# Attention steps laid between triples of matrix products, with order edges, and an add moved to the vector engine

## Chip, cores and metric

The kernel runs on one core of one Trainium2 chip. The metric is the device time of one execution in microseconds (us). Three runs of the kernel before took 760.43, 761.77 and 764.90 us, median 761.77 us.

## What is computed

The kernel chains three blocks on 1152 tokens (2 sequences of 576) of width 512.

1. Causal attention, 8 heads of width 64, with a bias from a running sum of `max(s, 0)`:
   `scores = q·kᵀ/8 + min(-(cum_i - cum_j), 0)`, masked above the diagonal; `attn = exp(scores - max) / (sum + 1e-9)`; `attn·v`.
2. A mixture of 4 experts: `out += p[:, e] * (relu(x @ w1[e]) @ w2[e])`, with w1 512x1024 and w2 1024x512.
3. A gated block: `((x @ w_a) * (x @ w_b)) @ w_out`, inner width 1536.

All in 32-bit floats. The kernel splits each operand of a product into a high and a low part and sums three products on TensorE (high·high, high·low, low·high). Such a group of three is a *triple*.

## The kernel before

**Stages.** The attention's rows fall into four groups (`GROUPS`, line 37): rows 0 to 255 of the first sequence, the rest of the first, the first 320 rows of the second, the rest of the second. The experts' tokens fall into turns (`TURNS`, line 41): 0 to 255, 256 to 511, 512 to 767, 768 to 1151. Three things are emitted in this order: the attention of group 0 with the first four steps of group 1 (line 1035); then `run(beside, True)` (line 1106), four expert stages (experts 0 and 1 on turn 0, expert 1 on turns 1 and 2) with the attention of groups 1 to 3 between them; then, with the attention closed, `run(after, False)`, which does all the rest: the last turn of expert 1 (products named `psq`), the other experts and the gated block.

**Experts' units.** A stage has 8 first-layer units (`l1_unit`, line 280: 4 triples of 256 columns into one PSUM bank, then ReLU and the two parts) and 2 second-layer units (`l2_unit`, line 292: 8 triples of 512 columns into one bank, then `add_share`). A triple is issued by `mm3` (line 255). The units are laid so that the first unit of the next stage comes ahead of the second layer of the stage before (`pipelined`, line 872).

**Attention steps.** `seq` (line 785) lists 80 pairs of head and row tile: steps 0 to 15 are group 0, 16 to 39 group 1, 40 to 63 group 2, 64 to 79 group 3. `attn_step` (line 792) number n is software-pipelined: it issues on TensorE the transposes of tile n-3 (L644), the scores of tile n (L596, L597), and, where a head ends, the product with v of the head that ended at n-4 (L680); beside it the softmax of tile n-1 (L606 on VectorE, L621 on ScalarE), the norm of tile n-2 (1e-9 added at L631 on ScalarE, or L629 on VectorE in group 0; reciprocal L632 on VectorE; multiplication L633 on GpSimd) and the copies of the transposed tile n-3 (L659 on ScalarE, L661 on VectorE). At a head's first step it also prepares the next head (L557 to L565) and issues the loads of the one after (L547 to L549) and of v (L571) on SyncE's queue, on which the weights' loads (L149) stand too.

**Pace.** `run` keeps a clock of the experts' products: a triple of n columns costs 3(n/2400 + 0.013) us, so a first-layer unit 1.44, a second-layer unit 5.43, a stage 22.35 and all four 89.4 us. After each unit it advances the clock, lays weight loads and splits (`weight_step`, one per 4 us of that clock), and then lays as many attention steps as `lead` (line 1077) asks for: steps 20 to 43 evenly by their column count over clock 0 to 29.7, steps 44 to 67 over 29.7 to 52.1, steps 68 to 83 over 52.1 to 74.4.

**Order in the queues.** The order laid in the program is a rank, not the queue's order. At compile time a scheduler with a timing model of its own fills each engine's queue: of the instructions that this model takes to be ready it takes the one laid first. So an attention instruction whose inputs are not ready in the model is passed by products laid behind it, as far as buffers reach (three PSUM banks for the experts' products). On the chip each queue then runs in the order that was written.

Of the kernel before, what the change touches and what calls it, by code (L numbers as in the profile page):

```python
# [11 lines left out]
AF = mybir.ActivationFunctionType  # L12
ALU = mybir.AluOpType
# [6 lines left out]
P = 128  # L20
# [26 lines left out]
NT0 = 256  # L47

NFIRST = 4


@with_exitstack
def fused_kernel(ctx, tc, qT, kT, v, s, dp, w1, w2, wa, wb, wo, out):
    nc = tc.nc
# [13 lines left out]
    ident = const.tile([P, P], F32, name="ident")  # L68
# [123 lines left out]
    def split_piece(r, key, form, wide, src, j):  # L192
# [16 lines left out]
        else:  # L209
            nsplit[0] += 1  # L210
            lo_eng = nc.gpsimd if nsplit[0] % 2 or nsplit[0] <= NFIRST else nc.vector
            two = slice(2 * j, 2 * j + 2)
# [39 lines left out]
    hts = {}  # L252
    begun = set()

    def mm3(ps, w, x, first, last, more=False):

        (lh, ll), (rh, rl) = w, x
        for k, (l, r) in enumerate(((lh, rh), (lh, rl), (ll, rh))):
            nc.tensor.matmul(  # L259
                ps, lhsT=l, rhs=r, start=first and k == 0, stop=last and k == 2, skip_group_check=more  # L260
            )

    def cols(pair, *at):
        return tuple(t[(slice(None), *at)] for t in pair)
# [320 lines left out]
    def st_scores(j, i):  # L585
        t = j.t[i]
        q0 = j.tiles[i][0] - j.q0
        cuts = [0, t.n] if t.n <= 512 else [0, 320, t.n]
        t.ps = []
        for c0, c1 in zip(cuts, cuts[1:]):  # L590
            ps = ps_s.tile([P, c1 - c0], F32, tag="sc", name=f"sc{j.nm}_{i}")
            t.ps.append((ps, c0, c1))
            if j.gi == 0:
                nc.tensor.matmul(ps, lhsT=j.qh[:, q0 : q0 + P], rhs=j.kr[:, c0:c1], start=True, stop=True)
                continue
            nc.tensor.matmul(ps, lhsT=j.qh[:, q0 : q0 + P], rhs=j.ks[:, c0:c1], start=True, stop=False)  # L596
            nc.tensor.matmul(ps, lhsT=j.qb[:, q0 : q0 + P], rhs=j.kb[:, c0:c1], start=False, stop=True)  # L597

    def st_softmax(j, i):
        t = j.t[i]  # L600
# [24 lines left out]
    def st_norm(j, i):  # L625
        t = j.t[i]
        r = st_p.tile([P, 1], F32, tag="r", name="r")
        if j.gi == 0:
            nc.vector.tensor_scalar(out=t.l, in0=t.l, scalar1=1e-9, scalar2=None, op0=ALU.add)  # L629
        else:  # L630
            nc.scalar.activation(out=t.l, in_=t.l, func=AF.Copy, bias=1e-9)  # L631
        nc.vector.reciprocal(out=r, in_=t.l)  # L632
        (nc.gpsimd if j.gi else nc.vector).tensor_scalar(  # L633
            out=t.e, in0=t.e, scalar1=r, scalar2=1.0, op0=ALU.mult, op1=ALU.mult
        )

    def st_transpose(j, i):
        t = j.t[i]
        t.tp = []
        for c0, c1 in [(0, i + 1)] if i < 4 else [(0, 4), (4, 5)]:  # L640
            ps = ps_t.tile([P, c1 - c0, P], F32, tag="tr", name=f"tr{j.nm}_{i}")
            for c in range(c0, c1):
                k0 = j.tiles[c][0]
                nc.tensor.transpose(ps[:, c - c0, :], t.e[:, k0 : k0 + P], ident)  # L644
            t.tp.append((ps, c0, c1))

    def st_evac(j, i):
        t = j.t[i]
# [19 lines left out]
    def st_av(j):  # L668
        a = (j.h % 2) * D
        if j.gi == 0 and j.h % 2:  # L670
            ps = xpair[j.gi]
        else:
            ps = ps_a.tile([P, j.nr], F32, tag="av", name=f"av{j.nm}")
        mms = []
        for c in range(j.i1):
            o = max(0, j.tiles[c][1] - j.r0)
            for e in (j.eh, j.el) if j.gi else (j.eh,):
                mms.append((c, o, e))
        for m, (c, o, e) in enumerate(mms):
            nc.tensor.matmul(  # L680
                ps[:, o:] if j.gi else ps[a : a + D, o:],
                lhsT=j.vs[:, c, :],
                rhs=e[:, c, o:],
                start=(m == 0),
                stop=(m == len(mms) - 1),
            )
        c = D - a
        t0 = j.b * S + j.r0
        x = slice(t0, t0 + j.nr)
        if j.gi == 0:  # L690
            xpair[j.gi] = ps
            if j.h % 2:
                split(xh[j.h // 2][:, x], xl[j.h // 2][:, x], ps, nc.vector)
            return
        if j.h % 2 == 0:
            xpair[j.gi] = (
                x_p.tile([P, j.nr], F32, tag="xs", name="xs"),
                x_p.tile([P, j.nr], F32, tag="xt", name="xt"),
            )
        xs, xt = xpair[j.gi]  # L700
        nc.scalar.activation(out=xt[a : a + D, :], in_=ps[c : c + D, :], func=AF.Copy)
        nc.vector.tensor_tensor(  # L702
            out=xs[a : a + D, :], in0=ps[a : a + D, :], in1=xt[a : a + D, :], op=ALU.add
        )
        if j.h % 2 == 1:
            split(xh[j.h // 2][:, x], xl[j.h // 2][:, x], xs, nc.gpsimd)
# [8 lines left out]
    c0 = st_p.tile([NR, 1], F32, tag="c0", name="c0")  # L715
# [15 lines left out]
        out=cum[:, :NT0], data0=ones[:NR, :NT0], data1=sc[:, :NT0], initial=0.0,  # L731
        op0=ALU.mult, op1=ALU.add,
# [5 lines left out]
        out=causal[:, S - P :], in_=causal[:, S - P :], pattern=[[-1, P]], compare_op=ALU.is_ge, fill=MASKED,  # L738
# [6 lines left out]
    for base, cm in ((0, 1), (H - 1, -1)):  # L745
        nc.gpsimd.affine_select(
            out=pick, in_=pick, pattern=[[-cm * H, len(GROUPS)]], compare_op=ALU.is_ge, fill=0.0,
# [4 lines left out]
        out=cum[:, NT0:], data0=ones[:NR, NT0:], data1=sc[:, NT0:], initial=cum[:, NT0 - 1 : NT0],  # L752
        op0=ALU.mult, op1=ALU.add,
    )
    nc.vector.tensor_tensor_reduce(
        out=pick, in0=cum[:, D : D + 4 * P].rearrange("p (g c) -> p g c", c=P)[:, :, D],
# [8 lines left out]
    for j_ in range(3):  # L765
        in_order(nc.sync.dma_start(
            out=ckD[j_].rearrange("g h c -> (g h) c"), in_=ck3[j_].bitcast(F32)
# [18 lines left out]
    state = {"n": 0}  # L786
# [5 lines left out]
    def attn_step():  # L792
        n = state["n"]
        state["n"] += 1

        if x := at(n):
            j, i = x
            if i == j.i0:
                k = jobs.index(j)
                if k + 1 < len(jobs):  # L800
                    prep_job(jobs[k + 1])
                if k + 2 < len(jobs):
                    load_job(jobs[k + 2])
            st_enter(j, i)
        if x := at(n - 3):
            st_transpose(*x)
        if x := at(n):
            st_scores(*x)
        if x := at(n - 2):
            st_norm(*x)  # L810
        if x := at(n - 1):
            st_softmax(*x)
        if x := at(n - 4):
            j, i = x
            if i == j.i1 - 1:
                st_av(j)
        if x := at(n - 3):
            st_evac(*x)
        if x := at(n):
            j, i = x  # L820
            if i == j.i0:
                prep_v(j)
                k = jobs.index(j)
                if k + 1 < len(jobs):
                    load_v(jobs[k + 1])
# [6 lines left out]
    def close_attention():  # L832
        actx.close()
        open_pools(ctx, [("h2", 2), ("raw", 3), ("q", 2), ("cv", 1)])
        pools["late"] = True
        late_ps.append(ctx.enter_context(tc.tile_pool(name="ps_m2", bufs=5, space=PSUM)))
        for part_ in ("h", "l"):
            tq[part_] = ctx.enter_context(tc.tile_pool(name="tq" + part_, bufs=1)).tile(
                [P, 3, 2, SL], F32R, name="tq" + part_
            )  # L840
# [211 lines left out]
    n = [k for k, u in enumerate(after) if u[0] == ("w1", halves[1][1])][-1]  # L1052
# [11 lines left out]
    area = [0]  # L1064
# [5 lines left out]
    for n in (2, 3, 4):  # L1070
        us = sum(c for st in stages[:n] for part in expert_stage(*st) for _, c, _ in part)
        turn_t.append(us)
    SLACK = 15.0
    lead = []
    for g in range(3):
        u0 = lead[-1][1] if lead else 0.0
# [2 lines left out]
    PACE, LATE_PACE = 4.0, 3.0  # L1079
    clock = {"t": 0.0, "w": 0.0}  # L1080

    def run(units, attention):
        for k, cost, u in units:
            for key in keys_of(k):
                weights_to(key)
            u()
            for key in keys_of(k):
                used(key)
            if hold[0]:
                continue  # L1090
            clock["t"] += cost
            while clock["w"] < clock["t"]:
                clock["w"] += PACE if attention else LATE_PACE
                weight_step()
            if not attention:
                continue
            goal = state["n"]
            for u0, u1, s0, s1 in lead:
                if u0 < clock["t"]:
                    c = area[s0] + (area[s1] - area[s0]) * min(1.0, (clock["t"] - u0) / (u1 - u0))  # L1100
                    while goal < s1 and area[goal + 1] <= c + 1e-6:
                        goal += 1
            while state["n"] < goal:
                attn_step()

    run(beside, True)
    close_attention()
    run(after, False)


# [48 lines left out]
```

## Time and profile before

| | |
|---|---|
| median of three runs | 761.77 us |
| the profiled execution | 760.76 us |
| its span, first to last instruction | 759.0 us |
| TensorE (PE) busy | 719.9 us, 95% |
| VectorE (DVE) busy | 533.0 us, 70% |
| ScalarE (ACT) busy | 334.8 us, 44% |
| GpSimd (POOL) busy | 416.2 us, 55% |
| mean granted TensorE clock | 0.987 of full speed |

The profile is of one execution; 1.8 us lie outside its span. PE is TensorE's matmuls, PEld its weight loads, which overlap them. PEclk is the clock that TensorE was granted, 1.00 being 2.4 GHz and 0.50 being 1.2 GHz; a value between is a mean over a stretch that has both. In a row of the timeline or of a group, `ps<-wh,hh` names the tile written and the tiles read; `sc` is the scores, `tr` the transposes, `av` the product with v, `ps` the experts' products up to the end of the attention.

### The profile page before, as it was taken

Reading aid. Unit: us, or ns where it says so; the run is one execution under the profiler, and the core shown is the slowest. Engines: PE = TensorE matmul, PEld = TensorE weight load, DVE = VectorE, ACT = ScalarE, POOL = GpSimd, SP = SyncE. Lnnn points to the kernel's source line nnn. Section 1 sums busy time; section 2 is a strip of 40 time slices with the busy share of each in tenths; the row PEclk is TensorE's granted clock in tenths of the full one; section 3 lists DMA queues with packets and bytes.
Section 4 is the critical chain, followed back from the end, with each engine's and each line's share of the span. In section 5 each row is a group of like instructions: output and inputs, shape, how many; then the busy total and the mean of one; then the engine's idle time right before and its main releaser. Section 6 shows DMA issues by size and latency. Waiting matters only on the chain.

```text
span 759.0 us, 11106 instructions
## 1 busy us (share of the span) xinstructions
PE 719.9 (95%) x3868; PEld 630.9 (83%) x3868; DVE 533.0 (70%) x1119; ACT 334.8 (44%) x756; POOL 416.2 (55%) x330
## 2 busy tenths in 40 slices
PE   5979897997998999999999999999899999999997
PEld 3678886886978888888888888888788888898896
DVE  7656857757759777776556657679874788887764
ACT  4667748868864432223312323243645324242410
POOL 1777735647634754333313344598466878788600
PEclk9999998999998999999999999999999999999999
DMA  6457323324402131211001112122102132213003
GB/s 192 136 184 228 91 68 90 100 74 127 120 18 84 55 100 41 81 57 57 31 25 56 56 57 74 65 84 87 53 29 86 62 103 68 95 63 104 5 1 125
DMA packets 35095, 61.34 MB, mean 81 GB/s; under 512 B 3472, under 2 KB 19376, under 8 KB 35040
## 3 DMA queue, kind: packets, MB, share of 16 engines
q1 hardware_dynamic: 34864, 60.50, 24.8%
q8 instruction: 31, 0.51, 0.3%
q14 instruction: 24, 0.20, 0.1%
q10 hardware_dynamic: 176, 0.14, 0.1%
HBM read 55.02 MB, written 2.58 MB: 76 GB/s over the span
## 4 chain that ended last, share of the span: by engine, by line
PE 55%; DVE 12%; POOL 8%; issue 4%; ACT 2%; DMA 1%; POOLq 0%; ACTq 0%; DVEq 0%; SPq 0%
PE ps L259 27%; PE psq L259 20%; PE pst L259 4%; POOL wl L74 3%; PE av L680 2%; POOL tp L155 1%; DVE tp L167 1%; PE tr L644 1%; DVE tp L163 1%; DVE h2l L74 1%; DVE acc L1027 1%; DVE tp L159 1%; POOL t L155 1%; DVE t L167 1%; DVE psq L405 1%
## 5 line engine op out<-in xcount | busy, mean ns | idle before, releaser
L259 PE MATMUL ps<-wh,h2h 128*128 128x512 f32 x332 | 130.6, 393 | 0.0
L259 PE MATMUL ps<-wl,h2h 128*128 128x512 f32 x332 | 129.6, 390 | 0.0
L74 POOL TENSOR_TENSOR wl<-raw,wh 128x1024 fp32r<-128x1024 f32 x24 | 58.5, 2448 | 125.5 <-ACT wh L73 95.4
L259 PE MATMUL ps<-wh,h2l 128*128 128x512 f32 x332 | 125.7, 392 | 0.8 <-DVE h2l L74 0.8
L307 DVE SCALAR_TENSOR_TENSOR acc<-ps,pr,acc 128x512 f32<-128x512 f32 x111 | 82.1, 745 | 40.4 <-PE ps L259 39.7
L259 PE MATMUL psq<-xh,wh 128*128 128x448 f32 (+1 forms) x224 | 82.9, 372 | 1.7 <-DVE xs L702 1.7
L259 PE MATMUL psq<-xl,wh 128*128 128x448 f32 (+1 forms) x224 | 82.6, 369 | 0.0
L259 PE MATMUL psq<-xh,wl 128*128 128x448 f32 (+1 forms) x224 | 82.6, 370 | 0.0
L259 PEld LDWEIGHTS ps<-wh,h2l 128*128 128x128 f32 x332 | 62.2, 188 | 14.7 <-DVE h2l L74 1.6
L259 PEld LDWEIGHTS ps<-wh,h2h 128*128 128x128 f32 x332 | 62.4, 188 | 11.8 <-ACT h2h L73 0.3
L259 PEld LDWEIGHTS ps<-wl,h2h 128*128 128x128 f32 x332 | 62.4, 188 | 11.1
L318 ACT ACTIVATE h2h<-psq 128x448 fp32r<-128x448 f32 (+1 forms) x56 | 29.5, 532 | 93.6 <-PE psq L259 74.3
L74 POOL TENSOR_TENSOR wl<-sums,wh 128x1024 fp32r<-128x1024 f32 x24 | 58.6, 2441 | 5.2 <-ACT h2h L318 2.7
L73 ACT ACTIVATE wh<-raw 128x1024 fp32r<-128x1024 f32 x24 | 25.5, 1062 | 69.7 <-PE ps L259 52.9
L633 POOL TENSOR_SCALAR e<-e,r 128x448 f32<-128x448 f32 (+4 forms) x64 | 39.9, 630 | 28.9 <-DVE r L632 27.5
L259 PE MATMUL psq<-tqh,wh 128*128 128x448 f32 x144 | 52.9, 368 | 0.9 <-DVE h2l L74 0.5
L606 DVE CUSTOM_DVE_ANT_0 e<-sc,causal 128x128 f32<-128x128 f32 (+3 forms) x80 | 35.6, 450 | 24.2 <-PE tr L644 13.8
L259 PE MATMUL psq<-tql,wh 128*128 128x448 f32 x144 | 52.6, 365 | 0.0
L259 PE MATMUL psq<-tqh,wl 128*128 128x448 f32 x144 | 52.5, 364 | 0.0
L621 ACT ACTIVATE e<-e,mn 128x128 f32<-128x128 f32 (+4 forms) x80 | 45.9, 574 | 11.6 <-DVE mn L606 9.1
L644 PE MATMUL tr<-ident,e 128*128 128x128 f32 x240 | 45.2, 291 | 6.1 <-DVE el L661 4.1
L155 POOL TENSOR_SCALAR tp<-tp 128x512 f32<-128x512 f32 x24 | 47.4, 1995 | 5.9 <-ACT tp L154 5.9
(174 smaller groups left out, 1949.4 us busy)
## 6 DMA issues: line engine op xcount, KB each, us to landing
raw<-in_w SPq DMA_DIRECT2D x40, 512.0 KB
raw<-in_wa SPq DMA_DIRECT2D x12, 512.0 KB
raw<-in_wb SPq DMA_DIRECT2D x12, 512.0 KB
raw<-in_wo SPq DMA_DIRECT2D x12, 512.0 KB
kr<-in_kT SPq DMA_DIRECT2D x16, 288.0 KB
vr<-in_v SPq DMA_DIRECT2D x16, 160.0 KB
kb<-ks SPq DMA_DIRECT2D x16, 144.0 KB
out<-acc SPq DMA_DIRECT2D x9, 256.0 KB
```

The source lines that it names most:

```text
L73: nc.scalar.activation(out=hi, in_=src, func=AF.Copy)
L74: lo_eng.tensor_tensor(out=lo, in0=src, in1=hi.bitcast(F32), op=ALU.subtract)
L155: nc.gpsimd.tensor_scalar(out=t.bitcast(F32), in0=t.bitcast(F32), scalar1=2.0**-15, scalar2=GMAX, op0=ALU.max, op1=ALU.min,)
L167: nc.vector.scalar_tensor_tensor(out=t, in0=hi, scalar=-(1 << 30), in1=t, op0=ALU.bitwise_and, op1=ALU.bitwise_or,)
L259: nc.tensor.matmul(ps, lhsT=l, rhs=r, start=first and k == 0, stop=last and k == 2, skip_group_check=more)
L307: nc.vector.scalar_tensor_tensor(out=dst, in0=ps, scalar=share, in1=dst, op0=ALU.mult, op1=ALU.add)
L318: nc.scalar.activation(out=hh, in_=src, func=AF.Relu)
L606: nc.vector.tensor_tensor_reduce(out=t.e[:, c0:c1], in0=ps, in1=causal[:, m0 + c0 : m0 + c1], scale=-1.0, scalar=seed, op0=ALU.add, op1=AL ...
L621: nc.scalar.activation(out=t.e, in_=t.e, func=AF.Exp, bias=mn, scale=-1.0 if j.gi else -SCALE, accum_out=t.l)
L633: (nc.gpsimd if j.gi else nc.vector).tensor_scalar(out=t.e, in0=t.e, scalar1=r, scalar2=1.0, op0=ALU.mult, op1=ALU.mult)
L644: nc.tensor.transpose(ps[:, c - c0, :], t.e[:, k0 : k0 + P], ident)
L680: nc.tensor.matmul(ps[:, o:] if j.gi else ps[a : a + D, o:], lhsT=j.vs[:, c, :], rhs=e[:, c, o:], start=(m == 0), stop=(m == len(mms) - 1),)
```

## The change

- `run` no longer lays attention steps after a unit. Instead `mm3` itself advances the clock after each triple (`advance`) and lays the steps that are due there, in the middle of a unit. The cost of a triple and `lead` are as before.
- Each attention step records the names of its TensorE instructions: the second scores product, the last transpose, the last product with v. The first product of each later triple gets an order edge behind the instructions recorded by the third-last step laid (`LAG = 2`). The edge is on one engine and only fixes the order in its queue: no semaphore, no instruction.
- The recording and the edges end with `run(beside, True)`.
- In `st_norm` the 1e-9 is added on VectorE for all row tiles, not on ScalarE for groups 1 to 3.

```diff
+LAG = 2
...
+    passed, mixed = [], []
+    NOSYNC = mybir.DependencyInfo(mybir.DependencyClass.NoSync, mybir.DependencyReason.DATA)
+
     def mm3(ps, w, x, first, last, more=False):

         (lh, ll), (rh, rl) = w, x
         for k, (l, r) in enumerate(((lh, rh), (lh, rl), (ll, rh))):
-            nc.tensor.matmul(
+            ins = nc.tensor.matmul(
                 ps, lhsT=l, rhs=r, start=first and k == 0, stop=last and k == 2, skip_group_check=more
             )
+            if k == 0 and len(passed) > LAG:
+                for name in passed[-1 - LAG]:
+                    tc.add_manual_dep(ins.ins, name, NOSYNC, reason="the attention's pace")
+        if mixed:
+            mixed[0](3 * (rh.shape[-1] / 2400 + 0.013))
...
-            nc.tensor.matmul(ps, lhsT=j.qb[:, q0 : q0 + P], rhs=j.kb[:, c0:c1], start=False, stop=True)
+            ins = nc.tensor.matmul(ps, lhsT=j.qb[:, q0 : q0 + P], rhs=j.kb[:, c0:c1], start=False, stop=True)
+            passed[-1].append(ins.ins.name)
...
-        if j.gi == 0:
-            nc.vector.tensor_scalar(out=t.l, in0=t.l, scalar1=1e-9, scalar2=None, op0=ALU.add)
-        else:
-            nc.scalar.activation(out=t.l, in_=t.l, func=AF.Copy, bias=1e-9)
+        nc.vector.tensor_scalar(out=t.l, in0=t.l, scalar1=1e-9, scalar2=None, op0=ALU.add)
...
     def attn_step():
         n = state["n"]
         state["n"] += 1
+        passed.append([])
...
+    def advance(us):
+
+        clock["t"] += us
+        goal = state["n"]
+        for u0, u1, s0, s1 in lead:
+            if u0 < clock["t"]:
+                c = area[s0] + (area[s1] - area[s0]) * min(1.0, (clock["t"] - u0) / (u1 - u0))
+                while goal < s1 and area[goal + 1] <= c + 1e-6:
+                    goal += 1
+        while state["n"] < goal:
+            attn_step()
+
     def run(units, attention):
...
-            clock["t"] += cost
+            if not attention:
+                clock["t"] += cost
...
+    mixed.append(advance)
     run(beside, True)
+    mixed.clear()
+    passed.clear()
     close_attention()
```

## Rows read from the trace of the kernel before

**Rows 1.** The page: share of busy time, and the TensorE clock in 40 slices.
```profile
PE 719.9 (95%) x3868; PEld 630.9 (83%) x3868; DVE 533.0 (70%) x1119; ACT 334.8 (44%) x756; POOL 416.2 (55%) x330
...
PEclk9999998999998999999999999999999999999999
```

**Rows 2.** Stretches: length, busy PE, PEld, DVE, ACT, POOL, clock, DMA share.
```profile
20.00:62.40 42.40, 36.89 (x213) 30.31 (x212) 27.69 (x92) 27.18 (x74) 32.41 (x29) 0.96 0.54 173
62.40:113.70 51.30, 49.18 (x325) 44.89 (x324) 34.82 (x97) 34.07 (x93) 30.61 (x32) 1.00 0.36 111
113.70:140.60 26.90, 21.71 (x130) 18.77 (x128) 20.09 (x70) 22.78 (x80) 15.41 (x24) 0.87 0.31 89
140.60:169.80 29.20, 29.20 (x201) 26.75 (x200) 18.89 (x69) 20.26 (x77) 14.55 (x24) 1.00 0.30 87
169.80:197.90 28.10, 22.74 (x164) 20.09 (x164) 21.41 (x73) 25.09 (x79) 20.55 (x24) 1.00 0.46 131
197.90:231.50 33.60, 30.01 (x196) 26.30 (x195) 20.92 (x57) 20.16 (x54) 13.52 (x17) 0.99 0.16 43
```

**Rows 3.** The same view, two stretches that begin with the attention's last products.
```profile
220.00:240.00 20.00, 16.32 (x86) 14.79 (x85) 15.73 (x31) 8.20 (x21) 4.15 (x5) 0.83 0.27 87
...
233.00:500.00 267.00, 267.00 (x1314) 235.54 (x1314) 180.20 (x288) 84.51 (x126) 118.63 (x56) 0.99 0.18 60
```

**Rows 4.** TensorE's timeline at the attention's end: start, us, instruction, idle before it.
```profile
224.40 0.36 PE L680 MATMUL av<-eh,vs 128*128 128x256 f32 x1 [0.94 <-ACT eh L659]
...
231.59 0.69 PE L259 MATMUL psq<-xh,wh 128*128 128x384 f32 x1 [1.71 <-DVE xs L702]
232.08 0.52 PE L259 MATMUL psq<-xl,wh 128*128 128x384 f32 x1
...
239.15 0.34 PE L259 MATMUL psq<-xh,wh 128*128 128x384 f32 x1
```

**Rows 5.** TensorE's groups up to 62.4 us: experts' first products of triples, scores.
```profile
L259 PE MATMUL ps<-xh,wh 128*128 128x256 f32 x34 | 10.2, 342 | 3.2 <-DVE hl L287 3.2
...
L596 PE MATMUL sc<-ks,qh 128*128 128x320 f32 (+2 forms) x8 | 2.8, 352 | 0.0
...
L259 PE MATMUL ps<-wh,hh 128*128 128x512 f32 x6 | 2.3, 389 | 0.0
```

**Rows 6.** The same view from 62.4 to 113.7 us.
```profile
L259 PE MATMUL ps<-xh,wh 128*128 128x256 f32 x36 | 10.4, 292 | 0.8 <-DVE hl L287 0.8
L259 PE MATMUL ps<-wh,hh 128*128 128x512 f32 x26 | 10.3, 397 | 0.0
...
L596 PE MATMUL sc<-ks,qh 128*128 128x320 f32 (+2 forms) x20 | 7.2, 360 | 1.3 <-DVE mn L606 1.2
```

**Rows 7.** The same view from 140.6 to 169.8 us.
```profile
L259 PE MATMUL ps<-xh,wh 128*128 128x256 f32 x26 | 7.4, 285 | 0.0
...
L259 PE MATMUL ps<-wh,hh 128*128 128x512 f32 x16 | 6.3, 395 | 0.0
...
L597 PE MATMUL sc<-kb,qb 67*128 67x128 f32 (+2 forms) x12 | 3.4, 285 | 0.0
```

**Rows 8.** The same view from 169.8 to 197.9 us.
```profile
L596 PE MATMUL sc<-ks,qh 128*128 128x320 f32 (+2 forms) x16 | 5.6, 370 | 1.7 <-POOL ks L564 0.7 <-POOL vs L74 0.6 <-DVE mn L606 0.3
...
L259 PE MATMUL ps<-xh,wh 128*128 128x256 f32 x19 | 4.8, 287 | 0.0
```

**Rows 9.** The add by line: duration ns min/median/max; then VectorE's group of line 287.
```profile
L629 DVE TENSOR_SCALAR l<-l x16: 126/146/155, 11.9 to 34.3; 128x1 f32<-128x1 f32 x16
...
L631 ACT ACTIVATE l<-l x64: 184/197/232, 38.6 to 220.7; 128x1 f32<-128x1 f32 x64
...
L287 DVE SCALAR_TENSOR_TENSOR hl<-ps,hh 128x256 fp32r<-128x256 f32 x29 | 11.8, 417 | 1.6 <-ACT hh L286 1.0
```

**Rows 10.** Timelines of GpSimd and TensorE: one tile's norm, and its transposes.
```profile
90.76 0.64 POOL L633 TENSOR_SCALAR e<-e,r 128x448 f32<-128x448 f32 x1 [1.05 <-DVE r L632]
...
104.06 0.62 PE L644 MATMUL tr<-ident,e 128*128 128x128 f32 x4
```

**Rows 11.** SyncE's queue: weight loads ahead of a head's key load.
```profile
41.74 6.54 SPq L149 DMA_DIRECT2D raw<-in_w  x3
48.38 0.38 SPq L548 DMA_DIRECT2D kr<-in_kT  x1
```

**Rows 12.** TensorE's timeline in the first unit: products of one bank, out of program order.
```profile
25.84 0.70 PE L259 MATMUL ps<-xl,wh 128*128 128x256 f32 x3
...
29.24 0.71 PE L259 MATMUL ps<-xh,wh 128*128 128x256 f32 x3
```

More of the change, by code (lines that the diff above doesn't have):

```diff
@@ L643, in st_transpose @@
                 k0 = j.tiles[c][0]
-                nc.tensor.transpose(ps[:, c - c0, :], t.e[:, k0 : k0 + P], ident)
+                ins = nc.tensor.transpose(ps[:, c - c0, :], t.e[:, k0 : k0 + P], ident)
             t.tp.append((ps, c0, c1))
+        passed[-1].append(ins.ins.name)
     def st_evac(j, i):
@@ L679, in st_av @@
         for m, (c, o, e) in enumerate(mms):
-            nc.tensor.matmul(
+            ins = nc.tensor.matmul(
                 ps[:, o:] if j.gi else ps[a : a + D, o:],
@@ L686, in st_av @@
             )
+        passed[-1].append(ins.ins.name)
         c = D - a
@@ L1094, in run @@
                 weight_step()
[L1095 to L1104, printed above, removed]
+    mixed.append(advance)
     run(beside, True)
+    mixed.clear()
+    passed.clear()
     close_attention()
```

## The prediction, made before the change was run

> **What bounds the kernel now.** I read the page first, then TensorE's stretches, the groups of each stretch, and the timelines around the gaps. The page says TensorE is busy 95% of the span [rows 1], so what can be won is its idle time and its half-speed clock. From 233 to 500 us it is busy 267.00 of 267.00 us [rows 3]: whatever is gained before the attention's end reaches the end of the kernel in full. After that point the weights' chain follows TensorE's release of buffers, so I let it move along and cost nothing.
>
> The stretches [rows 2] are cut where the attention and the experts change roles. Up to 113.7 us the experts run ahead of the attention. By 62.4 us, when step 22 issues its scores, 34 triples of 256 columns and 6 of 512 are done [rows 5]; at the code's own price (0.120 and 0.226 us a product) that is 34x3x0.120 + 6x3x0.226 = 16.3 us of products, where the pace lays step 24 at 7.1 (column count 2368 of 9856, times 29.7 us). In the next stretch they do 36 and 26 more [rows 6], 13.0 + 17.6 = 30.6 us, beside 20 scores products, that is 15 steps. Then the experts have nothing left that does not need the attention's rows, and from 113.7 to 140.6 us the attention runs nearly alone: PE is busy 21.71 of 26.90 us at a mean clock of 0.87 [rows 2]. The same comes back from 169.8 to 197.9 us (22.74 of 28.10), and at the end the attention's tail stands alone, with 1.71 us of waiting for its last copy [rows 4]; the first products of the last turn then run at 1.2 GHz (one each 0.32 us, from 232.08 on; the row at 239.15 is at full speed), clock 0.83 over 220 to 240 us [rows 3, 4].
>
> The attention is late because of the order in TensorE's queue, and not because its data are late: a tile normed at 91.40 us is transposed at 104.06 [rows 10], with PE busy 49.18 of 51.30 us and no other engine above 68% [rows 2].
>
> **The change part by part.** All sums are against the profiled execution, 760.8 us, 1.0 below the median of 761.8.
>
> *The handovers go.* With the edges no triple may start before the third-last step's products have been issued, so the experts lead by two or three steps at most; by the pace 15 us of products (89.4 - 74.4) are left when the attention ends, which cover its tail. What can go at most: idle 5.2 + 5.4 + 3.6 us in the three handovers (length less PE busy [rows 2]), clock (1 - 0.87)x26.9 = 3.5 and (1 - 0.83)x20 = 3.4 us [rows 2, 3]. Sum 21.1 us. I take all of it, and charge what the pace costs separately. What is late next in each handover is the attention step itself.
>
> *The early hold.* At 62.4 us the experts may stand at 7.1 and not at 16.3 us, so up to 9.2 us of products are pushed out of a stretch in which step 22 comes no sooner: its head's key load stood on SyncE's queue behind three weight loads that took 6.54 us [rows 11], and POOL was busy 32.41 of 42.40 us [rows 2]. The edge binds only the first of a triple's three products. The others of an open bank may still pass, as the first unit shows, where three products of the second kind run ahead of three of the first [rows 12]; in a 512-column unit that is up to 16x0.226 = 3.6 us, in a 256-column one 1.0 us. Bounds 0 (the attention comes as much sooner as the experts are held) and 9.2; I take 7, the upper end less the mean of the two allowances (2.3).
>
> *The paced middle of group 1, steps 22 to 43.* TensorE's work per step: (49.18 - 30.6)/15 = 1.24 us for the attention [rows 2, 6] and 29.7/24 = 1.24 for the experts, 2.48 in all. VectorE's: 34.82/15 = 2.32, plus the add of 0.15 [rows 9], less 0.12 for the 0.8 us fewer products (half of them first-layer, one 0.417 us copy for each 1.44 us [rows 9]) = 2.35. No engine works without gaps where the attention sets the pace: the busiest one there, ACT, reached 22.78/26.90 = 0.85 and 25.09/28.10 = 0.89 [rows 2]. At 0.87 VectorE needs 2.70 us a step, so PE waits 0.22 a step, 22 steps: 4.8 us. Bounds: 0 (TensorE is the slower), and 20.7 (a step as slow as in the stretch now, 51.3/15 = 3.42). I take 4.8, because the transposes' wait for the queue [rows 10] is what goes away.
>
> *Group 2, steps 44 to 67.* TensorE: (29.20 - 26x3x0.120 - 16x3x0.226)/12 = 0.75 [rows 2, 7], plus 22.35/24 = 0.93: 1.68. VectorE: 18.89/12 = 1.57, plus 0.15, less 0.11: 1.61, at 0.87 1.85. 0.17x24 = 4.1 us; bounds 0 and, with the present 29.2/12 = 2.43 a step, 18.0.
>
> *Group 3, steps 68 to 83.* TensorE: (22.74 - 19x3x0.120)/10 = 1.59 (16 scores products are 10 to 11 steps [rows 8]), plus 22.35/16 = 1.40: 2.99. VectorE: 2.14 + 0.15 + 0.11 more for the products = 2.40, at 0.87 2.76. TensorE is the slower: 0. Bound above: at the share that VectorE itself reached there, 21.41/28.10 = 0.76, it needs 3.16, and 0.17x16 = 2.7 us.
>
> *The add.* It takes 64x0.197 = 12.6 us from ACT and gives VectorE 64x0.146 = 9.3 [rows 9]; its price is in the two terms above. Left on ACT, VectorE would need 2.53 and 1.68 us a step and ACT (34.07/15 - 0.11)/0.87 = 2.48 and (20.26/12 - 0.10)/0.87 = 1.83: waits of 1.1 and 3.6 us in place of 4.8 and 4.1. The Trainium skill (Perfetto Trace Analysis, Optimizing Scalar/DVE Operations) advises the opposite direction, from VectorE to ScalarE, where VectorE is saturated; by that rule this edit alone gives 4.2 us away. VectorE is at 68% in the stretch from 62.4 us and ACT at 66% [rows 2], so the trace of before does not say yet that VectorE is the saturated one.
>
> *At nothing:* the edges (no instruction), and the moved steps' DMAs: five per head on SyncE's queue, now half a unit sooner beside the weights' loads, with the DMA engines at 0.16 to 0.46 from 62.4 us on [rows 2]. They hide behind the head that is computed meanwhile; without that cover a held key load costs what the early hold shows. Weight steps stay at the ends of units.
>
> Sum: 21.1 - 7 - 4.8 - 4.1 = 5.2 us gained, 760.8 - 5.2 = 755.6, at the median 756.6.
>
> **Rivals.** (a) *TensorE starves behind the edges.* Its queue is in order, so a triple behind a late transpose waits with it, and with it all experts' work. If a step of group 1 stays at 3.42 us, that term is 20.7 and not 4.8, and the time is 756.6 + 15.9 = 772.5. It decides from 3.10 us a step on (0.40x22 = 8.9 us more, 765.5). For it: the queues of VectorE, ACT and POOL are ordered by a model that had the attention late; POOL at 76% and the held load early on [rows 2, 11]. Against: 12.7 us between norm and transpose [rows 10].
>
> (b) *Gain and price cancel.* The full 9.2 early, and engines at 0.83 in place of 0.87: 2.83 and 1.94 a step, 7.7 and 6.2 us. 21.1 - 9.2 - 7.7 - 6.2 = -2.0, about 763.8. The same comes out if the two unbound products of each triple let the experts pass as now; then 761.8.
>
> (c) *The pace costs nothing once group 1 is under way*, because the three engines do fill up: 21.1 - 7 = 14.1, 747.7. For it: DVE's share of 0.68 at present leaves room. Against: no stretch of the attention has any engine beside TensorE above 0.89.
>
> **How the numbers follow.** Chances: forecast 0.34, (a) 0.30, (b) 0.22, (c) 0.14. A measurement of this kernel tells about 0.5% (3.8 us) from no change. The forecast and (c) are faster: 0.48; (b) is the same: 0.22; (a) is slower: 0.30. The range runs from a little under (c)'s time to that of (a), 744 to 772; the likeliest case's own range is 750 to 760, its two wait terms halved or one of them doubled.
>
> **What would show it.** Right: by 62.4 us the experts have done some 8 us of products; between 113 and 200 us no stretch in which PE is below 85% busy; 12 to 15 us of `ps` products after the last `av`; no idle before the first `psq` and its clock at 1.00; gaps before `ps` of under 0.5 us each, spread over 60 to 160 us and released by VectorE or ACT. Wrong: a step of group 1 over 3.1 us with PE idle before transposes or scores (a); the experts again 10 us ahead at 113 us (b); clock rows at 0.5 inside the paced stretch, which would add 1.7 us for each 3.4 us.

## The result, and the profile after

The changed kernel takes 751.14 us (median of 4 runs, 749.86 to 753.25), the kernel before 761.1 in the same series: ratio 0.9875, 95% interval 0.9835 to 0.9915. Once more, beside other kernels: 0.9867 (0.9835 to 0.9899). The forecast of 756.6 us had the sign, the main mechanism (the handovers fill up) and half of the gain: 5.2 us forecast, 10.0 measured. The profiled execution took 749.86 us, 10.9 less than the one before; its span is 748.0 us.

The page first: shares of busy time, and the clock in 40 slices.

```profile
PE 714.3 (95%) x3868; PEld 628.3 (84%) x3868; DVE 538.7 (72%) x1183; ACT 329.6 (44%) x692; POOL 414.6 (55%) x330
...
PEclk9789999999999999999999999999999999999999
```

VectorE has 64 instructions more and ScalarE 64 fewer, which is the add [rows 1]. The slices with a clock under 0.9 have moved to the first 56 us. Then TensorE by the stretches of before, the last one cut where the attention's neighbours end (length; busy PE, PEld, DVE, ACT, POOL; clock; DMA share).

```profile
20.00:62.40 42.40, 36.36 (x204) 29.41 (x203) 34.55 (x116) 30.80 (x81) 36.86 (x32) 0.84 0.56 178
62.40:113.70 51.30, 44.35 (x278) 40.03 (x278) 38.73 (x121) 37.24 (x90) 35.44 (x37) 0.93 0.44 130
113.70:140.60 26.90, 26.90 (x197) 25.27 (x196) 23.18 (x103) 22.83 (x79) 17.89 (x30) 1.00 0.38 102
140.60:169.80 29.20, 27.96 (x211) 26.47 (x211) 22.68 (x87) 25.04 (x72) 20.00 (x26) 1.00 0.45 125
169.80:197.90 28.10, 28.10 (x189) 25.72 (x189) 20.12 (x70) 19.96 (x51) 15.96 (x20) 1.00 0.31 85
197.90:223.00 25.10, 23.78 (x153) 21.33 (x152) 18.78 (x40) 10.05 (x24) 4.84 (x6) 1.00 0.22 70
```

Against [rows 2] it reads like an exchange. The two handovers in the middle are gone: 26.90 of 26.90 us with 197 matmuls where 21.71 with 130 stood, and 28.10 of 28.10. In their place the stretch up to 62.4 us has a clock of 0.84 (0.96 before), and the stretch from 62.4 to 113.7 us has 6.95 us of idle TensorE where it had 2.12, and a clock of 0.93. The attention's end, TensorE's timeline (start, us, instruction):

```profile
221.76 0.39 PE L264 MATMUL ps<-wh,hl 128*128 128x512 f32 x1
221.99 0.34 PE L264 MATMUL psq<-xh,wh 128*128 128x384 f32 x1
222.17 0.34 PE L264 MATMUL psq<-xl,wh 128*128 128x384 f32 x1
```

The first product of the last turn starts at 221.99 us and not at 231.59, without a gap and at 2.4 GHz (0.18 us from start to start; before, 0.32 [rows 4]). The last product with v is at 211.9 us, so 10 us of products covered its copies. Up to there 9.6 us are gained and the half-speed start behind it is another 3.4. Of these 13.0 us the profiled execution gives 2.1 back in the rest of the kernel; 1.0 is a single longer wait (1.30 us before a `psq` product at 543.95, where it was 0.30), the remainder is spread and not explained.

Two groups say where the experts stand: first products of triples, and scores products, up to the scores of step 40 (109.5 us).

```profile
L264 PE MATMUL ps<-xh,wh 128*128 128x256 f32 x49 | 16.3, 332 | 0.0
L606 PE MATMUL sc<-ks,qh 128*128 128x320 f32 (+2 forms) x32 | 11.2, 358 | 2.7 <-POOL ks L574 2.7
L264 PE MATMUL ps<-wh,hh 128*128 128x512 f32 x16 | 6.7, 420 | 0.0
```

The same 32 scores products had 70 and 32 triples beside them in the kernel before, up to 121.6 us. At the code's price that is 28.5 us of products against 46.9: 18.4 us were kept for later.

What TensorE waits for now, from 20 to 223 us (line waited for: us in total, times, longest):

```profile
PE tr L652 <- DVE l L639: 4.0, 2, 2.9
PE sc L606 <- POOL ks L574: 2.7, 1, 2.7
PE sc L607 <- DMA kb<-ks: 2.4, 2, 2.1
PE tr L652 <- DVE el L670: 2.2, 6, 0.6
...
PE av L689 <- ACT eh L668: 1.6, 2, 1.2
```

The longest, 2.93 us, in the timelines of TensorE, VectorE and ScalarE:

```profile
97.68 0.52 PE L652 MATMUL tr<-ident,e 128*128 128x128 f32 x3 [2.93 <-DVE l L639]
...
93.84 2.44 DVE L222 TENSOR_TENSOR wl<-raw,wh 128x512 fp32r<-128x512 f32 x2 [2.44 <-ACT wh L220]
96.20 0.74 DVE L315 TENSOR_SCALAR acc<-ps,pr 128x512 f32<-128x512 f32 x1
96.86 0.68 DVE L670 TENSOR_TENSOR el<-tr,eh 128x512 fp32r<-128x512 f32 x1
97.46 0.14 DVE L639 TENSOR_SCALAR l<-l 128x1 f32<-128x1 f32 x1
...
97.78 0.28 DVE L640 RECIPROCAL r<-l 128x1 f32<-128x1 f32 x2
...
91.81 1.99 ACT L220 ACTIVATE wh<-raw 128x1024 fp32r<-128x1024 f32 x2
```

VectorE stood idle for 2.44 us until ScalarE had the high part of a weight, split the weight for 2.44 us, and only then came to an expert's sum and to the copy (L670) of the tile transposed before, which frees that tile's PSUM. The profile names the add of 1e-9 (L639) as what ended the wait. It runs at 97.46 us, right behind that copy, and the reciprocal that uses its result starts at 97.78, after the transposes have begun at 97.68. So it can't be their input, and I take the copy for what they waited for. This wait is weights' work lying in front of the attention's in a queue, not an engine that is full: VectorE is busy 38.73 of 51.30 us there, 0.755. The next two (2.7 us for a head's key on GpSimd, 2.1 for its DMA) are the preparation of a head.

### The profile page after: what moved, and what is told of

Its sections match the earlier page's. It is cut to its first block, busy times and chain, and to the rows that moved or that the text cites. A ratio compares the mean times of both kernels' runs of the same rounds, so it can differ in the third digit from the quotient of the medians.

```text
span 748.0 us, 11127 instructions
## 1 busy us (share of the span) xinstructions
PE 714.3 (95%) x3868; PEld 628.3 (84%) x3868; DVE 538.7 (72%) x1183; ACT 329.6 (44%) x692; POOL 414.6 (55%) x330
## 4 chain that ended last, share of the span: by engine, by line
PE 75%; DVE 11%; POOL 5%; DMA 4%; issue 3%; ACT 2%; SPq 0%; POOLq 0%; ACTq 0%; DVEq 0%
PE ps L264 35%; PE psq L264 24%; PE pst L264 6%; PE av L689 4%; PE tr L652 3%; POOL wl L76 2%; PE sc L604 1%; DMA raw<-in_w 1%; PE sc L607 1%; PE sc L606 1%; DMA kb<-ks 1%; POOL t L157 1%; POOL tp L157 1%; DVE t L169 1%; DMA kr<-in_kT 1%
## 5 line engine op out<-in xcount | busy, mean ns | idle before, releaser
L264 PEld LDWEIGHTS ps<-wh,h2h 128*128 128x128 f32 x332 | 62.4, 188 | 11.9 <-ACT h2h L75 0.4
L264 PEld LDWEIGHTS ps<-wl,h2h 128*128 128x128 f32 x332 | 62.4, 188 | 11.0
L264 PE MATMUL pst<-xh,wh 128*128 128x256 f32 x160 | 45.3, 283 | 2.7 <-DVE xl L76 2.7
```

The costliest lines, as they stand in the source:

```text
L264: ins = nc.tensor.matmul(ps, lhsT=l, rhs=r, start=first and k == 0, stop=last and k == 2, skip_group_check=more)
```

## The experiments

Each is measured against the kernel before, run beside it. For "lead" I counted the experts' products queued ahead of a step's scores, at the code's price, less the clock at which the pace lays that step; the kernel before has 12 us at step 22, 19 at step 40, 23 at step 64. "Reaches the last turn" is the start of the first `psq`.

**The add alone.**

```diff
-        if j.gi == 0:
-            nc.vector.tensor_scalar(out=t.l, in0=t.l, scalar1=1e-9, scalar2=None, op0=ALU.add)
-        else:
-            nc.scalar.activation(out=t.l, in_=t.l, func=AF.Copy, bias=1e-9)
+        nc.vector.tensor_scalar(out=t.l, in0=t.l, scalar1=1e-9, scalar2=None, op0=ALU.add)
```

> The kernel before with the 1e-9 added on VectorE for all row tiles; nothing else changed. My theory (the order of TensorE's queue carries the gain; the attention waits for that queue and not for VectorE or ScalarE) expects no change that can be measured: 757 to 765 us, with the experts still about 10 us of products ahead at step 20 and the handovers idle as before. Rival 'ScalarE was the bound of the attention': ScalarE loses 12.6 us of work, the handovers shorten, 751 to 756 us.

757.41 us, ratio 0.9972 (0.9948 to 0.9996): about 2 us faster, just clear of nothing and short of what the rival asked. The lead is unchanged (19.1 us at step 40). In its profile (756.02 us) the first handover has 4.3 us of idle TensorE and not 5.2, its clock is 1.00 and not 0.87, and the last turn is reached at 227.4 us, 4.2 sooner than in the kernel before.

**The pace alone**: the changed kernel with the add back on ScalarE.

```diff
-        nc.vector.tensor_scalar(out=t.l, in0=t.l, scalar1=1e-9, scalar2=None, op0=ALU.add)
+        if j.gi == 0:
+            nc.vector.tensor_scalar(out=t.l, in0=t.l, scalar1=1e-9, scalar2=None, op0=ALU.add)
+        else:
+            nc.scalar.activation(out=t.l, in_=t.l, func=AF.Copy, bias=1e-9)
```

> The changed kernel with the add back on ScalarE for groups 1 to 3. By the working of the prediction (VectorE the fuller engine under the pace) it is faster than the changed kernel by up to 4.2 us: about 747 us. Rival 'ScalarE is the fuller one': slower than the changed kernel by 3 us or more, 754 us or above. If the add hardly matters: 749 to 753 us.

752.34 us, ratio 0.9900 (0.9872 to 0.9927), against 0.9875 and 0.9867 with the add. The pace brings about 7.8 us alone. The move costs nothing, let alone the 4.2 us of the prediction's working; whether it adds a microsecond or two to the pace these intervals don't tell. The profiles say more. With the add back on ScalarE the last turn is reached at 226.78 us, without a gap and at full speed:

```profile
226.78 0.34 PE L264 MATMUL psq<-xh,wh 128*128 128x384 f32 x1
226.96 0.34 PE L264 MATMUL psq<-xl,wh 128*128 128x384 f32 x1
```

With it on VectorE this comes at 221.99 us and, in the second profile of the changed kernel, at 222.4. So of the 9.6 us gained up to there the pace alone has 4.8, and the add is worth 4.4 to 4.8 there, about what it brings by itself (4.2). Steps 22 to 43 take (121.20 - 55.85)/22 = 2.97 us each with the add on ScalarE and 2.84 with it on VectorE.

**The laying without the edges.**

```diff
-LAG = 2
+LAG = 10**6
```

> The changed kernel without the order edges: steps still laid between triples, add on VectorE. My theory (the edges bind, the laying alone leaves the scheduler free to pass the attention) expects the experts again 8 us or more ahead of the pace and idle handovers: 757 to 765 us. Rival 'the finer laying does it': 749 to 754 us with the experts within 3 us of the pace.

759.05 us, ratio 0.9981 (0.9957 to 1.0004), against 0.9972 for the add alone. The same first handover as before, and beside the 32 scores products up to 118 us the same 70 and 32 triples:

```profile
113.70:140.60 26.90, 21.02 (x132) 18.49 (x130) 20.05 (x84) 20.33 (x64) 16.01 (x25) 0.87 0.33 89
```

```profile
L264 PE MATMUL ps<-xh,wh 128*128 128x256 f32 x70 | 20.6, 314 | 3.6 <-DVE hl L297 3.5
L264 PE MATMUL ps<-wh,hh 128*128 128x512 f32 x32 | 12.7, 398 | 0.0
```

Where the steps are laid in the program changes nothing by itself: the scheduler passes them all the same. The edges do not act on TensorE's queue alone, though: one scheduler fills all queues, and the loads and copies move with it. How much of the gain comes from the other queues' order no run separates.

**The edges with steps laid after each unit.**

```diff
-        if mixed:
-            mixed[0](3 * (rh.shape[-1] / 2400 + 0.013))
...
+            if attention:
+                advance(0.0)
```

> Edges kept, steps laid after each unit as in the kernel before (several steps may fall due at the end of one 5.43 us unit), add on VectorE. My theory (edges carry the gain) expects most of the gain, 749 to 755 us, with longer single waits of TensorE behind the batch of steps at the end of second-layer units. Rival 'both are needed': 757 us or more.

759.82 us, ratio 1.0008 (0.9986 to 1.0030). My theory fell: the edges alone bring nothing here. The lead is held (1.4 us at step 40), but the steps themselves are late, step 44 at 124.1 us and step 64 at 161.5, where the changed kernel has 116.5 and 148.0. A 5.43 us unit makes four steps due at once in group 1, six or seven in group 2; with LAG 2 the next unit's first triple then stands behind all but the last two of them, with nothing between.

**LAG 0.**

```diff
-LAG = 2
+LAG = 0
```

> The changed kernel with LAG 0: a triple stands behind the last step laid, so the scores just laid and the transposes of the tile three steps back must be queued first. My theory (the edge has to leave the attention's chain from scores to transposes the time of some steps) expects longer waits of TensorE: 756 to 768 us, with TensorE's idle time from 36 us to the first product of the last turn above 18 us (13.3 in the changed kernel). Rival 'any edge does, the transposes already wait three steps in the program': 749 to 753 us.

762.05 us, ratio 1.0022 (0.9996 to 1.0047): no gain, as expected. TensorE idles 19.3 us from 36 us to the first `psq` (13.3 in the changed kernel). The stretches that were to profit now starve from the start, and the clock goes with them (0.88 and 0.87):

```profile
20.00:62.40 42.40, 33.42 (x165) 25.53 (x164) 26.36 (x99) 24.57 (x68) 31.23 (x27) 0.88 0.52 164
62.40:113.70 51.30, 42.20 (x237) 36.86 (x236) 36.43 (x109) 35.38 (x83) 33.27 (x35) 0.87 0.43 121
```

A single wait for a head's key on GpSimd lasts 6.83 us, up to 47.64, where the changed kernel's longest one of this kind is 2.7. With LAG 0 the first `psq` comes at 225.4 us, but with 16 triples of 512 columns (10.9 us at the code's price) of the stages before still to do, which all other variants have behind them there.

**LAG 4.** The same line, 4.

> LAG 4. If the waits of the changed kernel in group 1 (12 us from 28 to 111 us) come from the edges, two more steps of room take part of them away: 745 to 750 us. If they come from the attention's own chain (its data late whatever stands before it): 750 to 754 us. If the experts' lead is what cost time before: 754 us or more, growing with LAG.

755.49 us, ratio 0.9954 (0.9923 to 0.9986), with runs from 751 to 761. Up to the attention's end it equals the changed kernel (it reaches the last turn at 222.0 us). Then it loses 2.20 us on a wait for an expert's sum on VectorE, which the changed kernel does not have:

```profile
241.71 0.47 PE L264 MATMUL ps<-wh,h2h 128*128 128x512 f32 x1 [2.20 <-DVE acc L315]
```

and a stretch at half speed right behind it. The time is that of the third outcome, but not its cause, since LAG 8 is faster: in the profile the loss lies behind the paced part (529.3 us from the first `psq` to the end, 526.1 in the changed kernel), in the order that the scheduler happened to write there. Why its runs spread by 10 us stays open.

**LAG 8.**

> LAG 8: the experts may lead by up to 8 steps (10 us of products in group 1, the lead of the kernel before). My theory expects the handovers to come back in part: 754 to 760 us. Rival 'the lead is harmless as long as it is bounded': 748 to 753 us.

750.17 us, ratio 0.9887 (0.9833 to 0.9942). The rival is right. The experts' lead is back to 11.5 us at step 22 (5.0 at step 40, 7.6 at step 64), yet the two handovers in the middle stay filled:

```profile
113.70:140.60 26.90, 26.61 (x180) 23.99 (x179) 23.46 (x102) 23.95 (x80) 18.92 (x31) 1.00 0.39 108
169.80:197.90 28.10, 26.98 (x202) 25.34 (x202) 22.93 (x76) 23.08 (x59) 18.12 (x21) 1.00 0.39 104
```

The third is not filled: no experts' products are left behind the last product with v at 220.87 us, and the first `psq` waits 1.71 us.

**No edges before step 26.**

```diff
-            if k == 0 and len(passed) > LAG:
+            if k == 0 and len(passed) > LAG and state["n"] >= 26:
```

> The changed kernel without edges on triples laid before step 26 (clock under 8.1 us of products), to size the early hold. The prediction had it at 7 us. If the hold costs that, this kernel is faster than the changed one by 4 us or more: 743 to 747 us. If the attention comes sooner by as much as the experts are held (step 22 came 8.5 us sooner in the changed kernel), the hold is free and this kernel is the same or slower: 750 to 756 us.

748.75 us, ratio 0.9862 (0.9825 to 0.9898), the same as the changed kernel (0.9875, 0.9867); it reaches the last turn at 222.6 us against 222.0. That is no proof for the whole hold, since the experts stand at 8.3 us of products when step 22 issues its scores, only 1.1 more than in the changed kernel. LAG 8 and LAG 16, with 15.6 and 16.6 us of products there (16.3 in the kernel before), show it better: they reach the last turn at 222.9 and 221.9 us, no sooner. The early hold costs nothing that the runs show.

**The changed kernel again.**

> The changed kernel once more, beside the three below: 749 to 754 us.

748.97 us, ratio 0.9867 (0.9835 to 0.9899), first `psq` at 222.4 us.

**LAG 16.**

> LAG 16: the experts may lead by 16 steps, 20 us of products in group 1, about the lead that the kernel before reached (17 to 24 us). Theory as it stands after LAG 8 (a bounded lead is harmless as long as it leaves products for the attention's last steps of each group; what costs is that the experts run out): the handovers come back and the gain is lost in great part, 755 to 761 us. Rival 'any edge helps, whatever its reach': 748 to 753 us.

750.57 us, ratio 0.9881 (0.9857 to 0.9905). My revised theory fell too: an edge this loose keeps the gain. The lead is 12 us at step 22 and 21 at step 64, nearly as in the kernel before; at step 40 it is 10, where that kernel had 19 and had run dry:

```profile
62.40:113.70 51.30, 49.57 (x340) 45.09 (x338) 39.87 (x137) 40.90 (x102) 36.53 (x39) 1.00 0.48 140
113.70:140.60 26.90, 26.76 (x191) 24.86 (x191) 22.52 (x91) 21.35 (x71) 16.11 (x27) 1.00 0.32 87
...
169.80:197.90 28.10, 25.53 (x184) 23.30 (x184) 22.07 (x78) 23.59 (x61) 19.69 (x22) 1.00 0.45 122
```

The second handover is back in half (2.57 us of idle against 5.36) and the third with its 1.71 us wait, but the first is filled, and from 62.4 to 113.7 us it loses neither to waits nor to the clock (49.57 us busy, 1.00, against 44.35 and 0.93).

**Coarse laying with LAG 5.**

```diff
-LAG = 2
+LAG = 5
```

on the kernel of the edges with steps laid after each unit.

> Edges with LAG 5, steps laid after each unit (the coarse laying with more room). If the coarse laying failed because up to four steps fall due at once and then stand ahead of all products, like a LAG of 0, three more steps of room give the gain back: 749 to 754 us. If the laying between triples is needed for itself: 757 us or more.

754.56 us, ratio 0.9952 (0.9926 to 0.9979). The time falls between the two outcomes (749 to 754, 757 or more). The last turn is reached at 222.7 us, as with the finer laying, so up to there three more steps of room give the gain back: the laying between triples is what lets a short LAG work. What this kernel lacks at the end it loses later, with 8.7 us of idle TensorE behind that point against 5.7.

**Edges on all three products.**

```diff
-            if k == 0 and len(passed) > LAG:
+            if len(passed) > LAG:
```

> The changed kernel with the edge on all three products of a triple. The prediction counted on the two unbound products passing (2.3 of 9.2 us early). If they do pass on the chip, this kernel is slower by 2 us or more: 753 to 758 us. If the queue keeps triples whole anyway: 749 to 753 us.

750.05 us, ratio 0.9885 (0.9848 to 0.9923): no difference. The two free products of a triple don't pass in a way that counts. No variant is clearly faster than the changed kernel; freeing the first steps is level with it.

## Why the prediction came out as it did

*What bounds the kernel* held. The gain made before the attention's end reached the end but for 2.1 us, and the attention's lateness was in the main the queues' doing: with the order alone changed (the add left on ScalarE) step 64 issues its scores at 152.6 us and not at 169.9, with the add moved too at 148.0, with the add alone at 166.4.

*The handovers go* (21.1 us at most) held nearly in full. From 113.7 us on, idle is 1.2 us up to 197.9, 1.3 in the last stretch, and the clock is 1.00. That is 18.5 of the 21.1 us (14.1 less 2.5 of idle, and 6.9 of clock). Behind the last product with v 9.5 us of experts' products were left, not the 12 to 15 that I had named, and they were enough.

*The early hold* is the term that was mis-sized: 7 us forecast, none measured. The experts stood at 7.2 us of products when step 22 issued its scores, close to what was worked out (7.1), but that was at 54.0 us and not at 62.4. I had held step 22 fixed, with a head's key load behind weight loads on SyncE's queue [rows 11]. That load came at 45.31 us and not at 48.38, and GpSimd's preparation of the key (L574, before L564) at 51.57 and not at 57.46. The lower bound, "the attention comes as much sooner as the experts are held", was the right end; LAG 8 and LAG 16, which don't hold the experts there, gain nothing by it.

```profile
45.31 0.33 SPq L558 DMA_DIRECT2D kr<-in_kT  x1
...
51.57 1.42 POOL L574 TENSOR_TENSOR ks<-kr,ks 64x576 fp32r<-64x576 f32 x1
```

The same preparation in the kernel before:

```profile
57.46 1.44 POOL L564 TENSOR_TENSOR ks<-kr,ks 64x576 fp32r<-64x576 f32 x1
```

*The paced middle of group 1*, 4.8 us forecast: idle from 62.4 to 113.7 us grew by 4.8, and 3.6 us of clock came on top, which I had named as a sign of failure and left out of the sum. The size of the idle time is right by luck, since the mechanism is not: I had VectorE full at 0.87; it is busy 0.755, and TensorE waits in a few places, behind a weight's split and head preparation in the queues of VectorE and GpSimd. The gaps that I had expected before `ps`, under 0.5 us each, are not there at all; all are before transposes, scores or products with v. Steps 22 to 43 took 62.5/22 = 2.84 us each against 2.70.

*Group 2*, 4.1 us forecast: not there. Steps 44 to 63 took 31.5/20 = 1.58 us, under the 1.68 that I had given TensorE alone, with 1.24 us of idle TensorE among them. *Group 3* was 0 and is 0.

*The add* was priced with the wrong sign: 4.2 us to be had by leaving it on ScalarE; left there the kernel is no faster, and in the profiles it reaches the last turn 4.4 to 4.8 us later. Alone the move gains 2. By the Trainium skill's rule (Perfetto Trace Analysis, Optimizing Scalar/DVE Operations) moving work from VectorE to ScalarE may make sense where VectorE is saturated. At 0.68 before and 0.755 after I take it as not saturated, so the rule says nothing against the move. Why the move gains is not shown; from 54 to 222 us VectorE waits 15.4 us for ScalarE's copies of transposed tiles (`eh`) with the add on ScalarE, and 7.3 with it on VectorE.

In sum 5.2 forecast, and 5.2 + 7 + 4.1 less 2.5 (handover idle that stayed), 3.6 (clock) and 2.1 (given back) leaves 8.1 of the 10.9 in the profile. This leaves out the stretch from 20 to 62.4 us, where the clock of 0.84 for 0.96 costs (0.96 - 0.84)x42.4 = 5.1 us and idle grew by 0.5. With it the terms come to 2.5, and 8.4 us of the gain stand in none of them. What is left beside idle time and clock is time that the profile calls busy. Up to the first `psq`, before and after:

```profile
0.00:231.59 231.59, 200.67 (x1248) 174.47 (x1248) 158.51 (x523) 158.03 (x479) 131.24 (x165) 0.98 0.39 117
```

```profile
0.00:221.99 221.99, 197.66 (x1248) 174.50 (x1249) 171.85 (x599) 153.83 (x417) 134.28 (x167) 0.95 0.44 129
```

Of the 9.6 us, 6.6 are idle time and 3.0 busy time of the same 1248 matmuls, although the time at 1.2 GHz among them grew from 10.2 to 20.5 us. So my starting point, that idle time and half-speed clock are what can be won, was too narrow. Busy time hides starving: between 113.7 and 140.6 us TensorE was busy 21.71 us for 130 matmuls before, and 26.90 for 197 after, 0.167 against 0.137 each. A lone matmul counts its whole duration as busy (0.36 us at 224.40 [rows 4], where matmuls in a row start every 0.12 to 0.23), so the handovers cost more than their idle time. How the 8.4 us divide among the stretches I can't say.

That the forecast came out near the result is in part luck: it charged 15.9 us for the pace, of which 7 and 4.1 were not there, and did not have the clock up to 62.4 us, nor the gain in busy time.

*The rivals.* (a), starving behind the edges, is real and depends on their reach: LAG 0 (3.22 us a step of group 1) and LAG 2 with coarse laying (3.03) are no faster than before, against 2.84 in the changed kernel. (b) is out, since the edges on all three products change nothing. (c) came closer than the forecast: 747.7 against 751.1.

The experiments correct one belief that stood behind all of it, that the experts must be held close to the attention. With the add on VectorE, any reach from 2 to 16 steps (2 only with steps laid between triples) gives a first `psq` between 221.9 and 222.9 us (220.1 with the edges on all three products). By the runs with LAG 16 and without edges, which differ in the reach alone, what must not happen is that the experts run dry while group 1 is unfinished. TensorE's work before the last turn is the same 1248 matmuls in all of these; it costs time where one of the two has nothing ready.

## What to carry to other kernels

Where a scheduler lets bulk work pass a latency-bound chain, look at what is left for the bulk work to do when the chain is the only thing running; an order edge with room of some steps keeps some. Here its reach, from 2 to 16 steps, hardly moved the point where the chain ends, and no room at all (LAG 0) lost the gain. What stands behind that point can still change with it: LAG 4 lost 3 us there. Lay the chain's steps as finely as the edge is short: a tight edge with steps in batches gains nothing. And when work is pushed out of a stretch, don't hold the other side's times fixed; what was delayed by the same queues moves up.

## What the runs showed of the hardware that was not expected

TensorE's half-speed time was not less with the gain. Up to its first `psq` the changed kernel ran 20.5 us at 1.2 GHz, most of it between 30 and 50 us, around the waits for the first heads (a clock of 0.67 there, and 0.84 up to 62.4 us where the kernel before has 0.96 [rows 2]), and the kernel before 10.2 us and 6.8 more at that product. With LAG 16 it was 10.2 us up to the first `psq` and 3.4 at it, and that product comes at 221.91 us against 221.99, the time in the end being the same within the intervals. The two kernels differ in more than the clock, so this is a hint and no proof: the clock of a stretch in which TensorE waits for others need not tell what it costs. At the head of a stretch in which TensorE is the bound, as at 231 us before, it does: products started every 0.32 us there, and every 0.18 at full speed.
